# Decay attention followed by a hard-swish MLP on one core: when v is split and loaded, where its maximum stands, and how the MLP's work is shared out over the heads

## The chip, the core and the metric

The kernel runs on one core of one Trainium2 chip. The metric is the device time of one execution in microseconds, the median over runs. The engines are TensorE (PE, with its weight loads as PEld), VectorE (DVE), ScalarE (ACT), GpSimd (POOL) and SyncE (SP), whose queue issues all of this kernel's DMAs. Each engine works through its own instruction stream in order and waits there for what other engines or DMAs owe it.

## What is computed

The reference, cut to what matters (batch 8, 8 heads, 576 tokens, head size 64; then 4608 tokens of width 512 through an MLP of width 2048):

```python
scores = scale * np.matmul(q, k.transpose(0, 1, 3, 2))
cum = np.cumsum(np.log(np.clip(f, 0.0001, 1.0)), axis=-1)
decay = cum[:, :, :, None] - cum[:, :, None, :]
scores = np.where(causal, -1000000000.0, scores + decay)
attn = softmax(scores)                       # max, exp, sum, divide
attn_out = np.matmul(attn, v)
x = attn_out.transpose(0, 2, 1, 3).reshape(B * S, H * D)
h = x @ w_in
g = h * np.clip(h + 3.0, 0.0, 6.0) / 6.0
out = g @ w_out
```

## The kernel before

One program does both halves at once. The attention goes head by head through a list `VH`: four entries of kind A (two heads of batch 0 each, their first 256 queries), eight of kind B (the rest of batch 0) and 56 of kind F, one head each, for batches 1 to 7. "Head 4 of batch 3" below counts both from 0. The MLP works on tiles of 512 tokens, nine in all; tile t needs x from batch t (576 tokens a batch, so a tile ends inside a batch or with it), and so cannot be finished before that batch's last head.

**A head of kind F.** POOL copies q and k (`parts`, tiles TQ and TK), SP copies parts of them (`rests`, L453 and L454, into T7 and T1), POOL subtracts (L455, L458). PE computes the scores in two halves (`rows`, L608 and L611, tile pn). VectorE adds the mask and takes the row maximum (L619, pp and MF), and forms the bias nb (L625). ScalarE takes exp (L631) and a rounded fp16 copy (L645, tile ring); VectorE and POOL subtract for the rest (L648, L654, L659). SP transposes each half by DMA (L666, tile pT). PE multiplies by v (`av`, L691 to L696, tile pav), VectorE divides (L727 to L729) and after two heads splits x into two fp16 halves (xhl, L735). One head later SP transposes these into `xT` (`x_move`, L755).

**v.** A batch's v is loaded into the one buffer `vst` (`load_v`: L359 twice for the first 64 rows of chunk 0, and L360 for the other four chunks of 128 rows). `v_scale` takes the largest absolute value on VectorE in two reduces (L365: chunks 0 to 2, chunks 3 and 4), squares it, joins the partitions on PE and makes a power of two of it. `v_split` then makes two fp16 halves for a pair of heads (L396 on ScalarE, L397 on VectorE). The next load may only overwrite `vst` when all four pairs of the batch are split.

**The MLP's queue.** `units` holds generators of work. `moe_tile` of a tile yields 16 `h_unit`s (12 matmuls L781 to L783 into ph; Relu on ScalarE L791, product on VectorE L794 into r, fp16 copy L795 on ScalarE, remainder L796 on VectorE, both into gT) and then four `out_unit`s (48 matmuls L803 to L805 into po, L814 on ScalarE, L815 to memory). The main loop calls `fill(1)` eight times per head; each adds `rates[0]` to a credit, and units are taken from the queue while there is credit. A whole tile is 64 credits. The rate is 0.6 during kind B, 0.45 in batch 1 and 1.02 from batch 2 on. `done` puts a tile into the queue, right after `x_move` of the last pair of a batch, which happens in the middle of head 1 of the next batch. What remains in the queue runs after the last head, and then tile 8.

**What sets the order.** The loop gives only the program's order. A scheduler then orders each engine's stream by priority and by a simulated timeline, so that an instruction without unfinished inputs may move ahead of earlier ones. `tc.issue_after(x)` ties instructions behind x on its engine; the load of v is tied so behind an early DMA. `keep_in_program_order(y)`, which the change uses, ties y behind the one instruction of its engine that the program gave just before it.

Of the kernel before, what the change touches and what calls it, by code (L numbers as in the profile page):

```python
# [20 lines left out]
def kernel(  # L21
# [10 lines left out]
    nc = tc.nc  # L32
# [3 lines left out]
    B = vS.shape[0]  # L36
    H = NHEAD // B
    NT, DM = out.shape
    DFF = w_in.shape[1]
    P = 128  # L40
# [5 lines left out]
    NFC = DFF // P  # L46
    TT = 512
# [34 lines left out]
    NQK, NL, NST = 3, 2, 3  # L82
    W_RATE = (8, 5, 4)
    H_COST = 1.05
    F_RATE = (0.6, 0.45, 1.02)
    PIN = 0
    PIN0 = 1
    LOW_W = 0
# [6 lines left out]
    QA = 256  # L95
    CA = QA // P
    VH = [("A", g) for g in range(NPAIR)] + [("B", n) for n in range(H)]
# [46 lines left out]
    def v_parts(b):  # L144
        return v0 if b == 0 else [vst[:, 0:3], vst[:, 3:]]
# [34 lines left out]
    def pow2_scale(pm, s_col, i_col, name):  # L180
        pool, tag = (ps_t, "tr") if SV < s_col < SV + B else (ps_m, "mm")
        pt = pool.tile([P, 512], F32, tag=tag, name=f"pt_{name}")
        nc.tensor.matmul(pt[:, 0:1], ones, pm, start=True, stop=True)
        yield
        e = p2.tile([P, 2], F32, tag="ee", name=f"e_{name}")
        nc.vector.tensor_scalar(e[:, 0:1], pt[:, 0:1], 2.0 ** -100, None, op0=ALU.max)
        ei = e.bitcast(I32)
        nc.vector.tensor_scalar(
            ei[:, 1:2], ei[:, 0:1], 24, 23, op0=ALU.logical_shift_right, op1=ALU.logical_shift_left
        )  # L190
        si = SC.bitcast(I32)
        nc.vector.tensor_scalar(
            si[:, s_col:s_col + 1], ei[:, 1:2], -1.0, float(204 << 23), op0=ALU.mult, op1=ALU.add
        )
        nc.vector.tensor_scalar(
            si[:, i_col:i_col + 1], ei[:, 1:2], 1.0, float(50 << 23), op0=ALU.mult, op1=ALU.add
        )
        yield

    def scol(c):  # L200
        return SC[:, c:c + 1]
# [160 lines left out]
    def v_scale(b):  # L362
        pm = p2.tile([P, 2], F32, tag="pm", name=f"vm{b}")
        for i, t in enumerate(v_parts(b)):
            nc.vector.tensor_reduce(  # L365
                pm[:, i:i + 1], t.rearrange("p c (h e) -> p (c h) e", e=D + 1)[:, :, 0:D],
                axis=AX.XY, op=ALU.max, apply_absolute_value=True,
            )
            yield
        nc.vector.tensor_tensor(pm, pm, pm, op=ALU.mult)  # L370
        nc.vector.tensor_tensor(pm[:, 0:1], pm[:, 0:1], pm[:, 1:2], op=ALU.max)
        yield from pow2_scale(pm[:, 0:1], SV + b, IV + b, f"v{b}")
# [15 lines left out]
    def v_split(g):  # L388
        b, hp = divmod(g, NPAIR)
        t = v16[:, g % NV16]  # L390
        if g < NPAIR + NV16:
            nc.vector.memset(t[:, :, :, D:D + 1], 1.0)
        for j in range(2):
            o = (2 * hp + j) * (D + 1)
            src = vst[:, :, o:o + D]
            nc.scalar.activation(t[:, :, j, 0:D], src, AF.Copy, scale=scol(SV + b))  # L396
            nc.vector.scalar_tensor_tensor(  # L397
                t[:, :, j, D + 1:VW], src, scol(SV + b), t[:, :, j, 0:D],
                op0=ALU.mult, op1=ALU.subtract,
            )  # L400

    def load_x(v):
        kind, n = VH[v]
        t = ST[v % NST]
        if kind == "A":
            nc.sync.dma_start(
                t[:, 0:2 * QA].rearrange("p (h s) -> p h s", h=2),
                qk[2 * n:2 * n + 2, :, 0:QA].rearrange("h p s -> p h s"),
            )
        else:  # L410
            nc.sync.dma_start(t, qk[n])

    def load_c(v):
        kind, n = VH[v]
        t = TK[v % NQK].bitcast(F32)[D:D + 2]
        if kind != "A":
            nc.sync.dma_start(t[:, 0:S], scr[n])
            if kind == "F":
                nc.sync.dma_start(TQ[v % NQK].bitcast(F32)[D + 2:D + 4, 0:S], scr[n])
        elif n >= 2:  # L420
            nc.sync.dma_start(
                t[:, 0:2 * QA].rearrange("r (h s) -> r h s", h=2),
                scr[2 * n:2 * n + 2, :, 0:QA].rearrange("h r s -> r h s"),
            )
        else:
            for h in range(2):
                d = nc.sync.dma_start(
                    t[:, h * QA:(h + 1) * QA], cs.bitcast(F32)[2 * n + h:2 * n + h + 1, :, 0:QA]
                )
            if PIN0:  # L430
                small.append(d.ins)
# [9 lines left out]
    def parts(v):  # L441
        i = v % NQK
        s = ST[v % NST]
        nq, nk, q0 = spans(v)
        one = dict(scalar1=1.0, scalar2=0.0, op0=ALU.mult, op1=ALU.add)
        nc.gpsimd.tensor_scalar(TK[i][0:D, 0:nk], s[D:, 0:nk], **one)
        nc.gpsimd.tensor_scalar(TQ[i][0:D, 0:nq], s[0:D, q0:q0 + nq], **one)
# [370 lines left out]
    def moe_tile(t, c0=0, c1=TT):  # L818
        for fc in range(NFC):
            j, new = divmod(fc, NFC // NG)  # L820
            if new == 0 and t < B and c0 == 0:
                while j not in w_in_done:
                    next(w_in_q, None)
                moe_scale_in(t, j)
            yield from h_unit(t, fc, c0, c1)
        if t == 0:
            for _ in wq:
                pass
        if t < B and c0 == 0:
            moe_scale_out(t)  # L830
        for s in range(c0 // P, c1 // P):
            yield from out_unit(t, s)
# [43 lines left out]

    units = []

    credit, rates = [0.0], [1.0]

    def w_step():
        with tc.high_priority(offset=-LOW_W):
            next(wq, None)

    def fill(k):
        credit[0] += k * rates[0]
        while credit[0] >= 1 and units:
            with tc.high_priority(offset=-LOW_M):
                r = next(units[0], 0)
            if r == 0:  # L890
                units.pop(0)
            else:
                credit[0] -= r
        credit[0] = min(credit[0], 1.0)

    def one(*a):
        yield from moe_tile(*a)

    def done(v):
        kind, n = VH[v]  # L900
        if kind == "A":
            if n == NPAIR - 1:
                units.append(one(0, 0, QA))
            return
        b, h = divmod(n, H)
        if h == H - 1:
            units.append(one(b, QA if b == 0 else 0, TT))
            if b == B - 1:
                units.append(one(B))

    prev = None
    pend_x = None
    vq = v_scale(0)
    for i, (kind, n) in enumerate(VH):
        b, h = divmod(n, H)
        if kind == "A":
            b = h = 0
        wn = W_RATE["ABF".index(kind)]
        rates[0] = F_RATE[0] if kind == "B" else F_RATE[min(b, 2)]
        ahead = i + 2 < NV  # L920
        if i + 3 < NV:
            load_x(i + 3)
        if ahead:
            load_c(i + 2)
        if b + 1 < B and h == 6:
            load_v(b + 1)
        if b and h % 2 == 1 and h < H - 1:
            v_split((n + 1) // 2)
        sg = rows(i) if kind == "F" else scores(i)
        front = ahead and VH[i + 2][0] != "F"  # L930
        next(sg)
        if i + 1 < NV:
            rests(i + 1)
        if ahead:
            parts(i + 2)
        fill(1)
        if b + 1 < B and h == 7:
            vq = v_scale(b + 1)
        next(vq, None)
        fill(1)  # L940
        ph = next(sg)
        if i + 1 < NV and VH[i + 1][0] != "F":
            max_rows(i + 1)
        for _ in range(wn // 2):
            w_step()
        fill(1)
        next(vq, None)
        next(sg, None)
        fill(1)
        if pend_x is not None:  # L950
            x_move(pend_x)
            done(pend_x)
            pend_x = None
        if front:
            natural(i + 2, 0)
        fill(1)
        if b + 1 < B and h == 7:
            for _ in vq:
                pass
            if b:  # L960
                v_split((n + 1) // 2)
        for _ in range(wn - wn // 2):
            w_step()
        next(sg, None)
        fill(1)
        if front:
            natural(i + 2, 1)
        fill(1)
        if prev is not None:
            av(*prev)  # L970
            if VH[prev[0]][0] == "A" or VH[prev[0]][1] % 2 == 1:
                pend_x = prev[0]
        if n == H:
            v_split(n // 2)
        fill(1)
        prev = (i, ph)
    rates[0] = 1.0
    av(*prev)
    fill(4)
# [40 lines left out]
```

## Time and profile before

| | |
|---|---|
| median of 3 runs | 1084.57 us (1083.75 to 1087.27) |
| profiled execution | 1083.28 us, span from first to last instruction 1081.5 us |
| mean granted TensorE clock | 0.982 of full |
| busy: PE, DVE, ACT, POOL | 1010.1, 719.7, 610.1, 413.1 us |
| DMA | 133.74 MB, 124 GB/s on average |

How to read it: busy time is time in which an instruction of the engine was under way. Matmuls are pipelined and their ends are modelled, so a PE that is busy all of a stretch may still have been a little slower than it could be; the granted clock, which a throttle sets, is given beside it as a share of full speed. In rows by time windows each engine's busy time stands with the number of its instructions in that window. "A <- B" in rows of waits says that A's engine stood still until B was finished; "issue" means that the profile shows nothing that it waited for.

### The profile page before, as it was taken

Reading aid. Unit: us, or ns where it says so; the run is one execution under the profiler, and the core shown is the slowest. Engines: PE = TensorE matmul, PEld = TensorE weight load, DVE = VectorE, ACT = ScalarE, POOL = GpSimd, SP = SyncE. Lnnn points to the kernel's source line nnn. Section 1 sums busy time; section 2 is a strip of 40 time slices with the busy share of each in tenths; the row PEclk is TensorE's granted clock in tenths of the full one; section 3 lists DMA queues with packets and bytes.
Section 4 is the critical chain, followed back from the end, with each engine's and each line's share of the span. In section 5 each row is a group of like instructions: output and inputs, shape, how many; then the busy total and the mean of one; then the engine's idle time right before and its main releaser. Section 6 shows DMA issues by size and latency. Waiting matters only on the chain.

```text
span 1081.5 us, 20281 instructions
## 1 busy us (share of the span) xinstructions
PE 1010.1 (93%) x7074; PEld 577.4 (53%) x7074; DVE 719.7 (67%) x1887; ACT 610.1 (56%) x1285; POOL 413.1 (38%) x505
## 2 busy tenths in 40 slices
PE   2799977988999999999999989999999999999998
PEld 2567854755555555555555545555555555444443
DVE  7869899876885688468865795689668841510520
ACT  4778656845764577356754674477447841621520
POOL 7344455335434445444544444454445420000000
PEclk9989989999999999999999999999999999999999
DMA  8866547767756666667576856675666651000001
GB/s 258 277 172 194 150 105 134 179 127 150 156 114 141 140 146 118 137 129 164 108 139 138 164 113 130 146 166 114 128 140 128 106 112 46 1 10 30 1 1 39
DMA packets 261650, 133.74 MB, mean 124 GB/s; under 512 B 229444, under 2 KB 231036, under 8 KB 261548
## 3 DMA queue, kind: packets, MB, share of 16 engines
q1 hardware_dynamic: 261548, 132.45, 54.7%
q8 instruction: 56, 0.92, 0.3%
q14 instruction: 46, 0.38, 0.1%
HBM read 47.93 MB, written 9.73 MB: 53 GB/s over the span
## 4 chain that ended last, share of the span: by engine, by line
PE 64%; DVE 12%; DMA 9%; issue 5%; ACT 5%; SPq 2%; POOL 2%; DVEq 0%; POOLq 0%; ACTq 0%
PE po L803 10%; PE po L804 10%; PE po L805 10%; PE ph L781 7%; PE ph L782 7%; PE ph L783 7%; DMA vst<-in_vS_dram 3%; PE pn L611 3%; PE pn L608 2%; DVE pp L619 2%; DVE ring L648 2%; DMA T<-TK 1%; DVE gT L796 1%; DMA w<-in_w_in_dram 1%; DVE r L794 1%
## 5 line engine op out<-in xcount | busy, mean ns | idle before, releaser
L781 PE MATMUL ph<-xT,w 128*128 128x512 f16 (+1 forms) x640 | 231.2, 363 | 14.5 <-DVE r L794 9.1
L782 PE MATMUL ph<-xT,w 128*128 128x512 f16 (+1 forms) x640 | 230.2, 363 | 0.0
L783 PE MATMUL ph<-xT,w 128*128 128x512 f16 (+1 forms) x640 | 230.0, 363 | 0.0
L631 ACT ACTIVATE pp<-pp,nb 128x192 f32<-128x192 f32 x280 | 138.5, 552 | 148.8 <-DVE nb L625 145.8
L804 PE MATMUL po<-w,gT 128*128 128x512 f16 x576 | 216.3, 381 | 6.1 <-DVE w L294 6.1
L805 PE MATMUL po<-w,gT 128*128 128x512 f16 x576 | 215.9, 381 | 0.0
L803 PE MATMUL po<-w,gT 128*128 128x512 f16 x576 | 213.6, 381 | 1.1 <-ACT o L814 0.8
L648 DVE TENSOR_TENSOR ring<-pp,ring 128x128 f16<-128x128 f32 (+2 forms) x216 | 131.5, 622 | 84.1 <-ACT ring L645 83.2
L791 ACT ACTIVATE r<-ph,bias_r,SC 128x256 f32<-128x256 f32 (+7 forms) x272 | 144.4, 570 | 28.6 <-PE ph L783 27.9
L794 DVE SCALAR_TENSOR_TENSOR r<-r,ph 128x512 f32<-128x512 f32 (+1 forms) x160 | 100.1, 627 | 88.9 <-ACT r L791 88.6
L458 POOL TENSOR_TENSOR T<-ST,T 64x576 fp32r<-64x576 f32 (+1 forms) x68 | 101.2, 1488 | 143.2 <-DMA T<-TK 133.4
L619 DVE CUSTOM_DVE_ANT_0 pp<-pn,W 128x192 f32<-128x192 f32 x280 | 122.9, 482 | 20.6 <-PE pn L611 16.6
L796 DVE TENSOR_TENSOR gT<-r,gT 128x512 f16<-128x512 f32 (+1 forms) x160 | 118.3, 743 | 27.4 <-ACT gT L795 26.6
L795 ACT CAST gT<-r 128x512 f16<-128x512 f32 (+1 forms) x160 | 91.8, 575 | 75.9 <-DVE r L794 75.8
L608 PE MATMUL pn<-TK,TQ 68*128 68x192 f32 x336 | 124.1, 383 | 5.8 <-issue 5.0
L611 PE MATMUL pn<-T,T 128*128 128x192 f32 x336 | 113.5, 368 | 4.3 <-POOL T L458 4.3
L645 ACT CAST ring<-pp 128x192 f16<-128x192 f32 x280 | 112.9, 452 | 0.0
L455 POOL TENSOR_TENSOR T<-ST,TQ 64x576 fp32r<-64x576 f32 (+2 forms) x68 | 97.6, 1435 | 24.8 <-PE pn L611 18.2
L654 POOL TENSOR_TENSOR ring<-pp,ring 128x128 f16<-128x128 f32 x96 | 61.5, 641 | 105.5 <-ACT ring L645 83.7
L782 PEld LDWEIGHTS <-w 128*128 128x128 f16 x640 | 62.7, 99 | 65.8 <-issue 20.9
L805 PEld LDWEIGHTS <-gT 128*128 128x128 f16 x576 | 56.8, 99 | 74.9 <-issue 13.7
L781 PEld LDWEIGHTS <-w 128*128 128x128 f16 x640 | 63.1, 99 | 62.2 <-issue 14.3
(136 smaller groups left out, 1703.4 us busy)
## 6 DMA issues: line engine op xcount, KB each, us to landing
ST<-in_qk_dram SPq DMA_DIRECT2D x64, 288.0 KB
T<-TK SPq DMA_DIRECT2D x64, 144.0 KB
out_dram<-o SPq DMA_DIRECT2D x36, 256.0 KB
ring<-in_w_out_dram SPq DMA_DIRECT2D x16, 512.0 KB
T<-TQ SPq DMA_DIRECT2D x56, 144.0 KB
vst<-in_vS_dram SPq DMA_DIRECT2D x7, 1040.0 KB
ring<-in_w_in_dram SPq DMA_DIRECT2D x9, 512.0 KB
w<-in_w_in_dram SPq DMA_DIRECT2D x7, 512.0 KB
```

The costliest lines, as they stand in the source:

```text
L608: nc.tensor.matmul(dst, TQ[i][0:D + 4, qs], TK[i][0:D + 4, a:e], start=True, stop=False)
L611: nc.tensor.matmul(dst, T7[j][:, qs], T1[j][:, a:e], start=False, stop=True)
L619: nc.vector.tensor_tensor_reduce(pp[:r, w:w + kw], pn[:r, o:o + kw], W[:r, 4 * P + r - kw:4 * P + r], 1.0, -3.0e38, ALU.add, ALU.max, accu ...
L631: nc.scalar.activation(x_, x_, AF.Exp, bias=nb[:r, e0 + x:e0 + x + 1], scale=0.125)
L648: eng.tensor_tensor(hl[:r, a:a + c * P], pp[:r, at[c] + 64:at[c] + kw], hl[:r, h0[c] + 64:h0[c] + kw], op=ALU.subtract,)
L781: nc.tensor.matmul(ph, w1[0][:, cc, fs_], xh, start=(cc == 0), stop=False)
L782: nc.tensor.matmul(ph, w1[0][:, cc, fs_], xl, start=False, stop=False)
L783: nc.tensor.matmul(ph, w1[1][:, cc, fs_], xh, start=False, stop=(cc == NCC - 1))
L791: nc.scalar.activation(r[:, a:e], ph[:, a:e], AF.Relu, bias=bias_r, scale=scol(A1 + NG * b + fc * NG // NFC))
L803: nc.tensor.matmul(po, gT[:, 0, fc, ts_], w2[:, fc, 0, :], start=(fc == 0), stop=False)
L804: nc.tensor.matmul(po, gT[:, 0, fc, ts_], w2[:, fc, 1, :], start=False, stop=False)
L805: nc.tensor.matmul(po, gT[:, 1, fc, ts_], w2[:, fc, 0, :], start=False, stop=(fc == NFC - 1))
```

## The change

Three things change in the order in which the program gives its work, and one in how much of the queue a head takes.

- v is split for pairs 1, 2 and 3 of a batch in heads 1, 2 and 4 (before: 1, 3 and 5), and the next batch's v is loaded in head 5 (before: 6).
- The two reduces of `v_scale` are each tied behind the VectorE instruction that the program gave just before.
- A tile of batches 1 to 7 joins the queue at the start of the next head, no longer in the head in which its last x is moved.
- From batch 2 on the rate is no longer 1.02, but what is left in the queue less 8 credits, shared evenly over the fills up to the next tile, held between 0.5 and 1.25.

```diff
-    F_RATE = (0.6, 0.45, 1.02)
+    F_RATE = (0.6, 0.45)
...
-            nc.vector.tensor_reduce(
+            most = nc.vector.tensor_reduce(
                 pm[:, i:i + 1], t.rearrange("p c (h e) -> p (c h) e", e=D + 1)[:, :, 0:D],
                 axis=AX.XY, op=ALU.max, apply_absolute_value=True,
             )
+            if b:
+                tc.keep_in_program_order(most)
...
+    credit, rates, left = [0.0], [1.0], [0.0]
+    TILE = NFC * 2 * H_COST + TT // P * NFC // 2 * (2.0 - H_COST)
+    RESERVE = 8.0
+    def queue(unit, columns):
+        units.append(unit)
+        left[0] += TILE * columns / TT
+    def even(h):
+        heads = (1 - h) % H + 1
+        return min(max((left[0] - RESERVE) / (8 * heads), 0.5), 1.25)
...
                 credit[0] -= r
+                left[0] -= r
...
-        if b + 1 < B and h == 6:
+        if b and h in (1, 2, 4):
+            v_split(n // 2 + 1 if h > 1 else (n + 1) // 2)
+        if b + 1 < B and h == 5:
             load_v(b + 1)
-        if b and h % 2 == 1 and h < H - 1:
-            v_split((n + 1) // 2)
+        if moved is not None:
+            done(moved)
+            moved = None
+        rates[0] = F_RATE[0] if kind == "B" else F_RATE[b] if b < 2 else even(h)
...
             x_move(pend_x)
-            done(pend_x)
+            if VH[pend_x][0] == "F":
+                moved = pend_x
+            else:
+                done(pend_x)
```

What this makes of the streams is shown at three places of batch 4; batches 3, 5 and 6 look alike. Lines of the changed kernel are two higher there (L619 becomes L621, L781 becomes L783, and so on). In the names, pp_39 and pT_39 belong to head 3 of batch 4, pp_40 to head 4, r_3_6 to tile 3, vm5 to the maximum of batch 5's v.

VectorE at the maximum over the next batch's v, before:

```order
L619 ISA pp_39_1_6104,MF1_109<-pn_39_1_6099,W_88 128x320
L619 ISA MF1_109 128x1
L619 ISA pp_39_1_6104,MF1_109<-pn_39_1_6099,W_88 128x448
L619 ISA MF1_109 128x1
L365 TENSOR_REDUCE vm5_6760<-vst_112 128x1 x2
L648 TENSOR_TENSOR ring0_123<-pp_39_0_6050,ring0_123 128x128
```

and now:

```order
L621 ISA pp_40_0_6120,MF0_108<-pn_40_0_6111,W_88 64x64
L621 ISA MF0_108 64x1
L796 SCALAR_TENSOR_TENSOR r_3_3_0_6096<-r_3_3_0_6096,ph_3_3_0_6037 128x512
L627 TENSOR_SCALAR nb_40_6110<-MF0_108 128x3
L798 TENSOR_TENSOR gT_116<-r_3_3_0_6096,gT_116 128x512
L365 TENSOR_REDUCE vm5_6673<-vst_112 128x1
L621 ISA pp_40_1_6175,MF0_108<-pn_40_1_6170,W_88 128x320
```

Both reduces stood together behind head 3's maxima; now the first stands between the two halves of head 4's (in batches 3 and 5 behind the second half), and the second, not shown, among head 7's rows.

SP at the load of that v, before:

```order
L666 DMA_TRANSPOSE pT_38_5858<-ring1_124 128x13x128
L411 DMA ST1_104<-in_qk_dram 128x576
L666 DMA_TRANSPOSE pT_38_5858<-ring2_125 128x12x128
L359 DMA vst_112<-in_vS_dram 64x520 x2
L360 DMA vst_112<-in_vS_dram 128x4x520
L755 DMA_TRANSPOSE xT1_118<-xhl_36_5838 128x2x64
```

and now:

```order
L668 DMA_TRANSPOSE pT_39_5923<-ring0_123 128x13x128
L419 DMA TK0_96<-decay_dram 2x576
L421 DMA TQ0_93<-decay_dram 2x576
L668 DMA_TRANSPOSE pT_39_5923<-ring1_124 128x12x128
L455 DMA T71_102<-TQ2_95 64x576
L456 DMA T11_100<-TK2_98 64x576
L360 DMA vst_112<-in_vS_dram 128x4x520
```

The small part of the load (L359, not in the second piece) stays behind head 2's transposes; the large part moved behind those of head 3 and two copies for a later head.

PE at the first matmuls of tile 3, before, in head 1 of batch 4 (v = 37):

```order
L608 MATMUL pn_37_1_5748<-TK1_97,TQ1_94 128x320
L611 MATMUL pn_37_1_5748<-T11_100,T71_102 128x320
L608 MATMUL pn_37_1_5748<-TK1_97,TQ1_94 128x448
L611 MATMUL pn_37_1_5748<-T11_100,T71_102 128x448
L781 MATMUL ph_3_0_0_5765<-xT0_117,w10_113 128x512
```

and now, in head 3 (v = 39):

```order
L610 MATMUL pn_39_0_5925<-TK0_96,TQ0_93 128x256
L613 MATMUL pn_39_0_5925<-T11_100,T71_102 128x256
L610 MATMUL pn_39_0_5925<-TK0_96,TQ0_93 64x64
L613 MATMUL pn_39_0_5925<-T11_100,T71_102 64x64
L783 MATMUL ph_3_0_0_5949<-xT0_117,w10_113 128x512
```

The tile starts nearly two heads later; the transposes of its last x stay where they were on SP, around head 1.

More of the change, by code (lines that the diff above doesn't have):

```diff
@@ L877 @@
     units = []
-    credit, rates = [0.0], [1.0]
+    credit, rates, left = [0.0], [1.0], [0.0]
[7 more added lines that the diff above has]
+        return min(max((left[0] - RESERVE) / (8 * heads), 0.5), 1.25)
     def w_step():
@@ L902, in done @@
             if n == NPAIR - 1:
-                units.append(one(0, 0, QA))
+                queue(one(0, 0, QA), QA)
             return
@@ L906, in done @@
         if h == H - 1:
-            units.append(one(b, QA if b == 0 else 0, TT))
+            queue(one(b, QA if b == 0 else 0, TT), TT - QA if b == 0 else TT)
             if b == B - 1:
-                units.append(one(B))
+                queue(one(B), TT)
     prev = None
-    pend_x = None
+    pend_x = moved = None
     vq = v_scale(0)
@@ L918 @@
         wn = W_RATE["ABF".index(kind)]
-        rates[0] = F_RATE[0] if kind == "B" else F_RATE[min(b, 2)]
         ahead = i + 2 < NV
@@ L976 @@
         prev = (i, ph)
+    if moved is not None:
+        done(moved)
     rates[0] = 1.0
```

## Prediction

> **What bounds the kernel now.** I read the page first, then the chain, then the heads by time windows, then waits, then single rows.
>
> ```profile
> span 1081.5 us, 20281 instructions
> PE 1010.1 (93%) x7074; PEld 577.4 (53%) x7074; DVE 719.7 (67%) x1887; ACT 610.1 (56%) x1285; POOL 413.1 (38%) x505
> PE po L803 10%; PE po L804 10%; PE po L805 10%; PE ph L781 7%; PE ph L782 7%; PE ph L783 7%; DMA vst<-in_vS_dram 3%; PE pn L611 3%; PE pn L608 2%; DVE pp L619 2%; DVE ring L648 2%; DMA T<-TK 1%; DVE gT L796 1%; DMA w<-in_w_in_dram 1%; DVE r L794 1%
> ```
>
> TensorE is busy 93% of the span and carries the chain; the one transfer with a share worth naming is the load of v, 3%. So moving matmuls about gains nothing: only time in which PE stands still, or runs at a lower clock, can be had back. I cut the trace at the first score matmul (L608) of heads, so that one row is one batch (1 to 6), then heads 0 to 6 of batch 7, then the rest. Columns: length, then busy us (instructions) of PE, PEld, DVE, ACT, POOL, granted clock, DMA share, GB/s.
>
> ```profile
> 135.80:236.90 101.10, 82.70 (x733) 57.67 (x732) 92.08 (x255) 65.34 (x144) 48.63 (x49) 0.95 0.67 139
> 236.90:347.50 110.60, 106.15 (x794) 59.30 (x791) 80.40 (x217) 68.07 (x148) 48.76 (x64) 0.97 0.66 139
> 347.50:457.90 110.40, 107.73 (x802) 59.15 (x801) 77.15 (x200) 64.44 (x140) 50.59 (x63) 0.98 0.65 133
> 457.90:567.20 109.30, 106.42 (x807) 59.09 (x805) 82.47 (x227) 68.72 (x149) 51.61 (x64) 1.00 0.65 136
> 567.20:680.60 113.40, 107.95 (x804) 59.21 (x803) 79.05 (x211) 66.83 (x145) 52.86 (x66) 0.98 0.66 138
> 680.60:788.40 107.80, 106.08 (x803) 58.65 (x801) 79.32 (x198) 64.51 (x140) 50.27 (x63) 1.00 0.66 137
> 788.40:879.50 91.10, 91.10 (x695) 50.53 (x694) 68.92 (x186) 60.62 (x132) 41.71 (x51) 1.00 0.62 124
> 879.50:1081.50 202.00, 197.52 (x992) 91.13 (x988) 52.51 (x91) 61.13 (x103) 2.00 (x3) 1.00 0.09 23
> ```
>
> Batches 3 to 6 hold the same work and differ by up to 5.6 us; batch 7, which loads no v, has no PE idle at all. Head by head only two differ: head 1 (first five rows, batches 3 to 7) and head 4 (next five).
>
> ```profile
> 362.70:373.30 10.60, 10.10 (x88) 6.07 (x86) 6.42 (x17) 5.27 (x13) 4.23 (x7) 1.00 0.54 121
> 473.30:485.30 12.00, 10.06 (x86) 6.05 (x85) 7.84 (x24) 6.35 (x14) 5.93 (x9) 1.00 0.55 129
> 582.40:594.70 12.30, 10.08 (x87) 6.03 (x86) 6.59 (x19) 6.01 (x14) 6.73 (x9) 1.00 0.60 145
> 695.80:705.70 9.90, 9.90 (x86) 5.97 (x85) 5.52 (x16) 4.56 (x11) 3.75 (x5) 1.00 0.55 107
> 803.80:813.70 9.90, 9.90 (x86) 5.97 (x85) 6.21 (x19) 5.29 (x12) 3.75 (x5) 1.00 0.35 79
> 399.70:417.60 17.90, 15.73 (x106) 8.20 (x104) 15.86 (x40) 13.33 (x29) 8.01 (x9) 0.90 0.55 101
> 511.80:526.70 14.90, 13.96 (x104) 7.60 (x103) 13.11 (x35) 11.87 (x27) 6.87 (x8) 1.00 0.55 117
> 621.10:640.10 19.00, 15.77 (x106) 8.12 (x104) 17.10 (x41) 13.38 (x30) 8.21 (x9) 0.91 0.48 100
> 732.20:748.10 15.90, 14.18 (x106) 7.70 (x104) 15.04 (x37) 12.53 (x28) 8.19 (x10) 1.00 0.67 125
> 840.20:854.00 13.80, 13.80 (x104) 7.51 (x103) 12.22 (x30) 11.12 (x26) 8.51 (x10) 1.00 0.73 126
> ```
>
> Against the undisturbed 9.9 us, head 1 loses 0.7 + 2.1 + 2.4 + 0 = 5.2 us; against 13.8 us, head 4 loses 4.1 + 1.1 + 5.2 + 2.1 = 12.5 us. What PE waited for from 270 to 880 us (first two rows), and DVE from 240 to 880 us (total, times, longest):
>
> ```profile
> PE ph L781 <- DVE r L794: 8.1, 5, 3.2
> PE ph L781 <- DMA xT<-xhl: 4.7, 3, 2.2
> DVE vm L365 <- DMA vst<-in_vS_dram: 11.2, 4, 4.2
> DVE vm L365 <- issue: 3.1, 1, 3.1
> ```
>
> Head 1 loses to the transposes of x, which the first matmuls of a new tile need; head 4 to VectorE, which holds r and gT back while its maximum over v waits for the load.
>
> In head 4 of batches 3 and 5 PE idles 17.90 - 15.73 = 2.2 and 3.2 us, and the granted clock of the whole head is 0.90 and 0.91: 17.9 x 0.10 = 1.8 and 19.0 x 0.09 = 1.7 us more. Idle plus clock is the loss. Idle of 0.9 to 1.9 us in one head left the clock at 1.00. [...]
>
> **The change, part by part.** Every engine executes the same set of instructions before and after, so it adds and removes no work; it moves it.
>
> *A tile joins the queue at the next head's start.* The first ph matmul of a tile moves from behind head 1's scores to behind those of head 3, while the transposes stay at head 1 on SP. Two heads of 12 us stand against waits of at most 2.2 us. The cover is the rest of the tile before, which the even share stretches over these heads; were it gone, the waits would return at 5.2 us. I take all 5.2. Bounds 0 and 5.2.
>
> *Load of v and its maximum.* This is not what the words of the change suggest. SP issues L359 where it did, behind head 2's pT, but L360, four fifths of the load, now stands a head later, behind both pT transposes of head 3 and two copies (L455, L456). The first of the two reduces moves from head 3's to head 4's L619 rows in batches 3 to 6; it is tied to one VectorE instruction, which itself stands in head 4. Only the second goes to head 7. So the race with the load stays; when does each arrive?
>
> ```profile
> L365 DVE TENSOR_REDUCE vm<-vst x14: 1208/1480/1753, 124.1 to 731.6; 128x1 f32<-128x1536 f32 x7, 128x1 f32<-128x1024 f32 x7
> ```
> ```profile
> 503.88 0.58 SPq L360 DMA_DIRECT2D vst<-in_vS_dram  x1
> 509.58 2.88 DVE L365 TENSOR_REDUCE vm<-vst 128x1 f32<-128x1536 f32 x2 [3.13 <-issue]
> ...
> 840.34 1.16 SPq L453 DMA_DIRECT2D T<-TQ  x1
> 841.54 0.59 SPq L454 DMA_DIRECT2D T<-TK  x1
> 842.23 1.83 SPq L666 DMA_TRANSPOSE pT<-ring  x1
> ...
> 840.07 1.12 DVE L648 TENSOR_TENSOR ring<-pp,ring 128x256 f16<-128x256 f32 x2
> 846.38 0.68 DVE L796 TENSOR_TENSOR gT<-r,gT 128x512 f16<-128x512 f32 x1
> 847.39 0.61 DVE L619 CUSTOM_DVE_ANT_0 pp<-pn,W 128x448 f32<-128x448 f32 x1
> ```
>
> Batch 4 gives the load's time: from L360's issue at 503.88 to the reduce at 509.58, 5.7 us. Batch 7 gives a clean head 3 to 4. L648 ends at 841.2; the transpose (1.83), the copies (1.16 and 0.59, less if the first finds its data) and gaps bring L360 to 844.2 to 844.9, its data to 849.9 to 850.6. VectorE reaches the reduce's new place at 847.1 (behind gT, batches 4 and 6) or 848.0 (behind L619, batches 3 and 5). It waits 1.9 to 3.5 us, middle 2.7, and then reduces 1.75 us: 4.45 us. Now it is (11.2 - 1.2 of batch 2 + 3.1) / 4 = 3.3 us of waiting and 2.9 of reducing: 6.2 us. That is 1.75 us shorter per batch, so PE's idle of 2.2, 0.9, 3.2 and 1.7 us shrinks to about 0.4, 0, 1.5 and 0, below the gaps that cost clock. Since in two batches the reduce now also stands ahead of head 4's own L619 pair, I put the remaining loss at 5 us rather than 2. Gain 7.5; bounds 0 (waits as now) and 12.5 (load in time). The second reduce, 1.2 us in head 7, meets landed data; VectorE was busy 12.2 of 13.8 us in batch 7's head 4, without a loss on PE, so a head has room for it and it costs nothing. If that slack were gone it is 4 x 1.2 = 5 us.
>
> *Splits of v at heads 1, 2 and 4.* On VectorE they stand within some rows of where they did, the last in head 2 as before: 0.
>
> *Even shares from batch 2 on.* Batch 2's eight heads take 294 of the queue's matmuls where they took 369; 84 more run behind the last head's first score, 978 for 894. The last row of the batches' table holds those 894 in 202 us, so 84 are at most 19 us there, at clock 1.00 as in full heads; moving them costs nothing by itself. But batch 2 is where heads run thin:
>
> ```profile
> 251.30:258.10 6.80, 6.80 (x71) 4.51 (x70) 4.80 (x17) 3.19 (x7) 3.69 (x6) 1.00 0.68 157
> 258.10:264.40 6.30, 5.68 (x33) 3.44 (x31) 5.49 (x14) 2.74 (x7) 4.08 (x6) 1.00 0.23 43
> 264.40:282.20 17.80, 14.10 (x96) 7.77 (x95) 12.48 (x30) 12.35 (x27) 7.26 (x10) 0.81 0.88 178
> ```
>
> Heads 1 and 2 with 18 queue matmuls each run full; then head 3 idles 3.7 us and runs at 0.81, 17.8 x 0.19 = 3.4: with head 2's 0.6, 7.7 us lost. Between the scores of heads 0 to 4 stood 54, 18, 18, 36 and 60 queue matmuls; now 15, 57, 18, 24 and 36. Thin heads remain, but in two places. I take 2 us as gained, near the existing loss; bounds +7.7 and -5.
>
> *Batches 0 and 1.* Rows shuffle by a few places and v is asked for some rows earlier; batch 1 is tied to VectorE, 92.1 of 101.1 us. I take 0, bounds 3 either way.
>
> Sum: the profiled execution took 1083.28 us, 1.3 below the median of 1084.57. 1083.3 - 5.2 - 7.5 - 2 = 1068.6; on the median's footing 1070.
>
> **Rivals.** *All stalls go* (load in time, batch 2 smooth): 1083.3 - 5.2 - 12.5 - 7.7 + 1.3 = 1059. For it: batch 7's clean heads. Against: the race worked out above.
>
> *The maximum waits as before*: L360 a head later, the reduce a head later, nothing won: 1083.3 - 5.2 - 2 + 1.3 = 1077, 1079 without batch 2's part. For it: the rows of the new order. Against: 1.2 us of reducing does leave head 4.
>
> *Batch 2 starves, and it is slower*: heads 0, 2, 3 and 4 each lose what head 3 loses now, 7.1 us, 28.4 in place of 7.7: 1083.3 + 20.7 - 5.2 - 7.5 + 1.3 = 1093. It decides once batch 2 loses over 7.7 + 12.7 = 20.4 us. For it: less filler, and idle of 3.7 us was followed by 0.81. Against: 6.8 and 6.3 us heads above. [...]
>
> A later load is part of none: L360 now passes copies that read what POOL writes.
>
> ```profile
> SPq L411 <- POOL T L458: 89.3, 37, 6.3
> SPq L454 <- POOL TK L446: 0.6, 1, 0.6
> ```
>
> The copies hardly ever waited for POOL (0.6 us); the load of q and k (L411), which did, stands behind L360.
>
> **How the numbers follow.** Forecast 0.50, own range 1064 to 1075; all stalls go 0.17; maximum waits as before 0.21; starving 0.07; some other wait that eats the gain 0.05, about no change. A measurement here tells 0.3%, 3.3 us, from no change: under 1081.3 is faster. Faster: 0.50 + 0.17 + 0.15 of the third = 0.82; same 0.06 + 0.05 = 0.11; slower 0.07. The range 1058 to 1081 leaves out starving, the last case and a few hundredths at each end.
>
> **What would show it.** Head 1 of batches 3 to 5 near PE's busy time, with no wait for xT; VectorE still waiting 2 to 3.5 us for vst in head 4 of batches 3 to 6, with PE idle under 1.5 us and clock 1.00 there; no such wait in batch 2; the stretch from the last head's first score longer by up to 19 us. It is wrong if those waits on vst are gone (then lower), if head 4 keeps clocks near 0.9, or if batch 2 loses over 10 us.

## The result, and the profile after

The change made the kernel slower: 1099.88 us median of 4 runs (1096.02 to 1102.07) against 1084.16 us (1082.56 to 1087.27) on the same chip, a ratio of 1.0141 with a 95% interval of 1.0115 to 1.0167. The prediction said 1070 us and faster. The profiled execution took 1102.07 us, 18.8 us more than that of before, and its span grew by as much. From its page, the span and the engines' busy time:

```profile
span 1100.3 us, 20286 instructions
...
PE 1018.9 (93%) x7074; PEld 582.7 (53%) x7074; DVE 729.8 (66%) x1887; ACT 611.4 (56%) x1285; POOL 411.1 (37%) x505
```

The shares of busy time hardly moved; they cannot show where 18.8 us went. The table by stages can: batches 1 to 6, heads 0 to 6 of batch 7, the rest, cut at first score matmuls (now L610) as in the prediction, with the same columns.

```profile
142.90:242.80 99.90, 82.37 (x732) 57.58 (x732) 91.20 (x246) 63.32 (x139) 49.57 (x49) 0.93 0.65 138
242.80:343.60 100.80, 92.47 (x718) 52.77 (x715) 79.50 (x219) 66.83 (x147) 51.88 (x65) 0.95 0.74 145
343.60:455.90 112.30, 106.20 (x801) 58.52 (x797) 82.17 (x212) 66.64 (x144) 50.29 (x65) 0.98 0.65 135
455.90:564.40 108.50, 107.77 (x803) 59.53 (x801) 79.38 (x208) 67.00 (x144) 51.71 (x65) 0.99 0.61 135
564.40:680.30 115.90, 109.50 (x807) 60.26 (x805) 82.47 (x215) 66.96 (x144) 49.92 (x63) 0.97 0.61 132
680.30:789.30 109.00, 106.81 (x805) 58.98 (x803) 81.11 (x211) 67.07 (x144) 49.37 (x64) 1.00 0.65 138
789.30:880.20 90.90, 90.90 (x693) 50.14 (x692) 66.00 (x181) 56.90 (x125) 39.74 (x50) 1.00 0.64 124
880.20:1100.30 220.10, 215.63 (x1076) 99.45 (x1072) 57.45 (x100) 66.92 (x115) 2.40 (x4) 1.00 0.09 24
```

Against before, row by row: the stretch ahead of batch 1 is 7.1 us longer, batch 1 1.2 shorter, batch 2 9.8 shorter, batches 3 to 6 differ by +1.9, -0.8, +2.5 and +1.2, batch 7 0.2 shorter, the end 18.1 longer. Together 18.8. The number behind PE's busy time is its instructions: batch 2 does 76 fewer, the end 84 more. To see what a head loses whatever its share, I use a line that heads without PE idle lie on (in batch 7 before, 9.9 us with 33 queue matmuls and 13.8 us with 51): length = 2.85 us + 0.2156 us x queue matmuls. What a head takes beyond it I call its loss; single thin heads, with 18 to 30 queue matmuls, come out up to 1.3 us below the line. By it batch 2, with 75 queue matmuls fewer, should have become 16.2 us shorter and lost 6.5 of that: its loss went from 8.2 to 14.7. Batches 3 to 6 lost 18.5 before and lose 25.2 now.

Head 1 of batches 3 and 5 (first two rows), then head 4 of batches 3 to 7:

```profile
356.80:370.00 13.20, 13.20 (x103) 7.29 (x101) 9.04 (x26) 6.13 (x13) 8.12 (x11) 1.00 0.63 126
578.50:592.90 14.40, 13.38 (x102) 7.29 (x101) 10.95 (x26) 6.12 (x13) 10.35 (x13) 1.00 0.71 167
396.40:413.50 17.10, 13.21 (x97) 7.09 (x95) 8.68 (x23) 7.98 (x18) 6.41 (x8) 0.93 0.71 172
512.10:524.00 11.90, 11.90 (x96) 6.72 (x95) 7.55 (x20) 6.40 (x14) 6.26 (x8) 1.00 0.76 199
620.70:639.30 18.60, 13.22 (x97) 7.09 (x95) 7.64 (x22) 7.49 (x17) 6.40 (x8) 0.92 0.70 165
735.10:748.60 13.50, 12.14 (x97) 6.83 (x95) 8.63 (x21) 6.40 (x14) 6.76 (x8) 1.00 0.81 199
844.10:855.20 11.10, 11.10 (x93) 6.38 (x91) 9.78 (x25) 8.70 (x20) 6.22 (x8) 1.00 0.32 65
```

Head 1 is full, or nearly (5.1 us of loss before, 1.2 now). Head 4 still stands still for 3.9 and 5.4 us in batches 3 and 5 and for 1.4 in batch 6, and its clock falls to 0.93 and 0.92. The waits of PE from 270 to 880 us, then VectorE's for v from 240 to 885 us:

```profile
PE ph L783 <- DVE r L796: 11.6, 5, 5.4
PE pav L693 <- DMA pT<-ring: 4.7, 4, 1.9
PE pn L613 <- POOL T L460: 2.8, 2, 2.2
PE pt_v L183 <- DVE vm L373: 2.4, 2, 2.2
```
```profile
DVE vm L365 <- DMA vst<-in_vS_dram: 22.7, 4, 8.8
```

The wait for xT is gone, that for r has grown from 8.1 to 11.6 us, and VectorE waits 22.7 us for v. Why, shows SP's queue in batch 3 and VectorE beside it (first column the start, second the duration, in brackets the idle time before):

```profile
388.98 1.54 SPq L359 DMA_DIRECT2D vst<-in_vS_dram  x2
390.60 0.54 SPq L817 DMA_DIRECT2D out_dram<-o  x1
391.24 6.83 SPq L757 DMA_TRANSPOSE xT<-xhl  x5
398.23 1.31 SPq L668 DMA_TRANSPOSE pT<-ring  x1
...
400.95 1.44 SPq L668 DMA_TRANSPOSE pT<-ring  x1
...
404.00 0.59 SPq L360 DMA_DIRECT2D vst<-in_vS_dram  x1
```
```profile
393.77 1.12 DVE L650 TENSOR_TENSOR ring<-pp,ring 128x256 f16<-128x256 f32 x2
...
402.76 0.08 DVE L621 DVE_READ_ACCUMULATOR2_ANT MF<- 128x1 f32 x1
409.46 1.22 DVE L365 TENSOR_REDUCE vm<-vst 128x1 f32<-128x1024 f32 x1 [6.61 <-DMA vst<-in_vS_dram]
410.59 0.68 DVE L796 SCALAR_TENSOR_TENSOR r<-r,ph 128x512 f32<-128x512 f32 x1
```

Five transposes of x hold SP for 6.8 us ahead of head 3's pT, and L360 stands behind that. VectorE is at the maximum at 402.8; L360 goes out only at 404.0, and its data are there 5.5 us later; r (L796) and with it PE stand behind the maximum. In batches 4 to 6 VectorE waits 3.4, 8.8 and 3.9 us in the same place.

The batches are not alike in this. From the end of head 3's last L650 to L360 it is 404.00 - 394.89 = 9.1 us in batch 3 and 10.9 us in batch 5, but 4.0 and 4.6 us in batches 4 and 6; head 4 loses 5.1, 6.7, 0 and 1.5 us. Batch 4 has the same five transposes, but SP is through with them 2.0 us before that L650 ends, and not 3.2 us behind it:

```profile
502.20 6.35 SPq L757 DMA_TRANSPOSE xT<-xhl  x5
...
514.48 0.59 SPq L360 DMA_DIRECT2D vst<-in_vS_dram  x1
```
```profile
509.41 1.12 DVE L650 TENSOR_TENSOR ring<-pp,ring 128x256 f16<-128x256 f32 x2
...
519.99 1.22 DVE L365 TENSOR_REDUCE vm<-vst 128x1 f32<-128x1024 f32 x1 [3.38 <-DMA vst<-in_vS_dram]
```

Why SP reaches them later in batches 3 and 5 was not settled. One more reading: the reduce in head 4 is the second (128x1024). The tie holds it behind one instruction of the MLP's queue, which itself runs heads early.

### The profile page after: what moved, and what is told of

The parts are those of the page before. It is cut to its first block, busy times and chain, and to the rows that moved or that the text cites. A ratio compares the mean times of both kernels' runs of the same rounds, so it can differ in the third digit from the quotient of the medians.

```text
span 1100.3 us, 20286 instructions
## 1 busy us (share of the span) xinstructions
PE 1018.9 (93%) x7074; PEld 582.7 (53%) x7074; DVE 729.8 (66%) x1887; ACT 611.4 (56%) x1285; POOL 411.1 (37%) x505
## 4 chain that ended last, share of the span: by engine, by line
PE 61%; DVE 11%; DMA 10%; ACT 6%; issue 6%; POOL 3%; SPq 2%; DVEq 0%; ACTq 0%; POOLq 0%
PE po L805 10%; PE po L806 10%; PE po L807 10%; PE ph L783 7%; PE ph L784 7%; PE ph L785 7%; PE pn L613 3%; PE pn L610 3%; DVE pp L621 2%; ACT pp L633 2%; DMA pT<-ring 2%; DVE ring L650 2%; DMA T<-TK 1%; DMA ring<-in_w_out_dram 1%; SPq L757 1%
## 5 line engine op out<-in xcount | busy, mean ns | idle before, releaser
L783 PE MATMUL ph<-xT,w 128*128 128x512 f16 (+1 forms) x640 | 228.8, 365 | 14.6 <-DVE r L796 14.0
L784 PE MATMUL ph<-xT,w 128*128 128x512 f16 (+1 forms) x640 | 227.9, 363 | 0.0
L785 PE MATMUL ph<-xT,w 128*128 128x512 f16 (+1 forms) x640 | 227.1, 363 | 0.0
L650 DVE TENSOR_TENSOR ring<-pp,ring 128x128 f16<-128x128 f32 (+2 forms) x216 | 136.4, 642 | 67.9 <-ACT ring L647 67.2
L796 DVE SCALAR_TENSOR_TENSOR r<-r,ph 128x512 f32<-128x512 f32 (+1 forms) x160 | 100.1, 626 | 109.0 <-ACT r L793 108.6
L621 DVE CUSTOM_DVE_ANT_0 pp<-pn,W 128x192 f32<-128x192 f32 x280 | 123.1, 482 | 28.0 <-PE pn L613 23.6
L610 PE MATMUL pn<-TK,TQ 68*128 68x192 f32 x336 | 128.7, 396 | 0.6 <-DVE MF L621 0.5
L613 PE MATMUL pn<-T,T 128*128 128x192 f32 x336 | 116.8, 374 | 6.3 <-POOL T L460 6.3
L784 PEld LDWEIGHTS <-w 128*128 128x128 f16 x640 | 63.2, 99 | 71.3 <-issue 22.3
L785 PEld LDWEIGHTS <-w 128*128 128x128 f16 x640 | 63.3, 99 | 66.6 <-issue 9.7
L783 PEld LDWEIGHTS <-w 128*128 128x128 f16 x640 | 62.3, 99 | 58.6 <-issue 11.6
```

The costliest lines, as they stand in the source:

```text
L610: nc.tensor.matmul(dst, TQ[i][0:D + 4, qs], TK[i][0:D + 4, a:e], start=True, stop=False)
L613: nc.tensor.matmul(dst, T7[j][:, qs], T1[j][:, a:e], start=False, stop=True)
L621: nc.vector.tensor_tensor_reduce(pp[:r, w:w + kw], pn[:r, o:o + kw], W[:r, 4 * P + r - kw:4 * P + r], 1.0, -3.0e38, ALU.add, ALU.max, accu ...
L650: eng.tensor_tensor(hl[:r, a:a + c * P], pp[:r, at[c] + 64:at[c] + kw], hl[:r, h0[c] + 64:h0[c] + kw], op=ALU.subtract,)
L783: nc.tensor.matmul(ph, w1[0][:, cc, fs_], xh, start=(cc == 0), stop=False)
L784: nc.tensor.matmul(ph, w1[0][:, cc, fs_], xl, start=False, stop=False)
```

## The experiments

Theory 1: the maximum, put into head 4 without a firm place, races the load there, and that costs. Rival 2: the even shares cost by themselves, by thin heads in batch 2 and by moved waits. Rival 3: the earlier splits hold ScalarE, and PE waits for that. The first four runs, the next four and the last three stood beside the kernel before on one chip each (1084.4, 1082.2 and 1082.8 us there); "loss" is the sum over batches 2 to 6 in the profiled execution, before 26.7 us, after 39.9.

**pin_only**: the kernel before, with the ties alone.

```diff
+            if b:
+                tc.keep_in_program_order(most)
```

> The kernel before with the two reduces of the maximum tied as in the change, nothing else. In its order both reduces of batches 3 to 6 stand at head 7 and the load stays behind head 2's transposes. Theory 1 (the race of the maximum with the load in head 4 is what costs): head 4 of batches 3 to 6 loses nothing, 12.5 us of the kernel before come back, about 1072 us. Rival 2 (thin filler is what costs): the queue's shares are as before, so about 1084 us less the idle of PE behind VectorE alone, 1076 us. Rival 3 (earlier splits hold ScalarE): nothing of it is here, no statement beyond 1084 us.

Measured 1070.68 us (1067.62 to 1072.07), ratio 0.9879 (0.9839 to 0.9919). Without the shares the ties do hold both reduces at head 7, the load stays behind head 2, VectorE never waits for v from 240 us on, and head 4 loses nothing in any batch. All that PE waits for from 230 to 870 us:

```profile
PE ph L783 <- DMA xT<-xhl: 4.7, 2, 2.6
PE pav L693 <- DMA pT<-ring: 1.9, 2, 1.2
PE pn L610 <- DVE MF L621: 1.0, 1, 1.0
```

So one part of the change is worth 13 us, and another spoils it.

**shares_only**: the kernel before, with the rates of `even(h)`. (`moved` is left out: beside the shares it changes no place in the program's order, since the queue then never runs dry from batch 2 on and `done` only adds to its end.)

```diff
-        rates[0] = F_RATE[0] if kind == "B" else F_RATE[min(b, 2)]
+        rates[0] = F_RATE[0] if kind == "B" else F_RATE[b] if b < 2 else even(h)
```

> The kernel before with the even shares alone. In its order L360 moves behind head 3's transposes and both reduces stand in head 4, as in the change. Theory 1: the waits on vst in head 4 grow to 3 to 9 us as in the change and cost 13 to 16 us in batches 3 to 6, the transposes of x cost nothing (5 us back): 1082 to 1086 us, and with 6 us lost in batch 2 up to 1092. Rival 2: batches 2 to 7 lose through thin heads wherever the maximum stands: 1095 us or more. Rival 3: no splits are moved, 1080 us.

Measured 1099.13 us, ratio 1.0149 (1.0115 to 1.0183): all of the change's cost. In the order L360 stands behind head 3's pT, both reduces in head 4. Theory 1 had set 1082 to 1086 us, at most 1092, and rival 2 1095 or more, so by the time rival 2 fits; but 25.1 of the 29.3 us lost in batches 3 to 6 are lost in their heads 4, where the maximum waits, and not in thin heads. VectorE's wait for v from 240 to 885 us and PE's largest from 230 to 870 us:

```profile
DVE vm L365 <- DMA vst<-in_vS_dram: 30.4, 5, 9.2
```
```profile
PE ph L781 <- DVE r L794: 22.5, 6, 8.1
```

**splits_only**: the kernel before, with the splits in heads 1, 2 and 4 and the load in head 5.

```diff
-        if b + 1 < B and h == 6:
+        if b and h in (1, 2, 4):
+            v_split(n // 2 + 1 if h > 1 else (n + 1) // 2)
+        if b + 1 < B and h == 5:
```

> The kernel before with the splits of v in heads 1, 2 and 4 and the load in head 5, nothing else. Load and maximum stand in batches 3 to 6 where they stood. Theory 1: 1084 us, 3 us either way for batch 1 and 2. Rival 2: 1084 us. Rival 3: waits of ScalarE's splits for pav grow from 12 to some 30 us and cost 5 to 10 us: 1090 us.

Measured 1083.29 us, ratio 0.9999 (0.9975 to 1.0022). Rival 3 is out for the splits by themselves.

**max_at_7**: the changed kernel, the second reduce tied behind the first and not behind a queue instruction. Both then stand at head 7.

```diff
+            if b and i == 0:
+                tc.keep_in_program_order(most)
+                first = most
+            if b and i == 1:
+                tc.add_manual_dep(most.ins, first.ins.name, ..., reason="behind_first")
```

> The changed kernel with one edit: the second reduce is tied behind the first, so that both stand at head 7. Theory 1: the waits on vst (22.7 us of VectorE in batches 3 to 6) vanish and 13 of the 15.7 us come back: 1087 us. Rival 2: only PE's idle behind VectorE (11 us in the heads 4) matters if filler was lacking anyway, so less than half comes back: 1094 us or more. Rival 3: no difference, 1100 us.

Measured 1085.02 us, ratio 1.0016 (0.9993 to 1.0038): 14.9 us below the changed kernel. No wait for v is left and head 4 loses at most 1 us in batches 3 to 6. But it is still 14 us above pin_only: batch 2 loses 15.9 us, and from 230 to 870 us PE now waits mostly for something else:

```profile
PE pav L700 <- DMA pT<-ring: 13.1, 11, 3.3
```

**shares_max_at_7** (the kernel before, the shares, both reduces at head 7) and **splits_max_at_7** (the kernel before, the splits, both at head 7), the tie as in max_at_7. The first, and the last two runs below, keep `moved`, which is without effect there.

> The kernel before with the even shares and with both reduces at head 7 (the second tied behind the first); splits and load are given as before. Theory 1 (what is left of the loss beside the race is thin heads at the start of batch 2, and these come from the splits' new places, which leave 15 queue matmuls in head 0): heads 0 to 4 of batch 2 hold 30, 21, 45, 33, 45, so batch 2 loses 3 to 6 us and the waits for xT are gone: 1068 to 1072 us. Rival 2 (the shares themselves cost, since 84 matmuls run behind the last head): 1080 to 1085 us, as with all parts.

> The kernel before with the new places of splits and load and with both reduces at head 7; the rate stays 1.02. Heads 0 to 4 of batch 2 hold 15, 57, 9, 93, 48 queue matmuls. Theory 1: batch 2 loses 12 to 16 us as in the change, batches 3 to 6 lose only what the waits for xT take (5 to 9 us): 1079 to 1084 us. Rival 2: no shares, so as with the ties alone, 1071 us.

Measured 1079.8 us (ratio 0.9986, 0.9956 to 1.0015) and 1070.58 us (0.9896, 0.9864 to 0.9928). The second is the changed kernel without its shares and `moved`, and as fast as pin_only; batch 2 loses 5.9 us, so by themselves the splits do not thin it, as theory 1 had it. The first is 9 us above pin_only: rival 2 holds for that much. Theory 1 missed both (1068 to 1072 and 1079 to 1084 us). Head 1 has no waits for xT any more, but head 4 of batches 4 and 6 has waits of 2.4 and 3.0 us for pT. SP's queue ahead of the first (the pT is head 3's, which PE multiplies by in head 4), and PE:

```profile
488.14 6.35 SPq L764 DMA_TRANSPOSE xT<-xhl  x5
...
495.09 1.47 SPq L675 DMA_TRANSPOSE pT<-ring  x1
...
498.73 1.51 SPq L675 DMA_TRANSPOSE pT<-ring  x1
```
```profile
504.19 0.20 PE L700 MATMUL pav<-v,pT 128*128 128x65 f16 x1 [2.43 <-DMA pT<-ring]
```

The wait for the transposes of x was not won but passed on: pT stands behind all five.

**ties_rate_040**: pin_only with 0.40 in place of 0.45 for batch 1, so that more of tile 0 is left to batch 2.

```diff
-    F_RATE = (0.6, 0.45, 1.02)
+    F_RATE = (0.6, 0.40, 1.02)
```

> The kernel before with the two ties of the change and a rate of 0.40 in place of 0.45 in batch 1. Batch 1 takes 15 queue matmuls fewer, which leaves heads 0 to 4 of batch 2 with 51, 39, 51, 45, 51 in place of 54, 18, 18, 36, 60. Theory 1: batch 2 loses 0 to 1 us where the ties alone lose 6.4, all else as there: 1064 to 1066 us. Rival 2: fewer queue matmuls inside the first batches mean more behind them, 1074 us.

Measured 1065.72 us (1060.96 to 1072.01), ratio 0.9852 (0.9802 to 0.9902): faster than both kernels and the lowest median here, though its interval overlaps that of pin_only. Batch 2 takes 51, 39, 51, 45, 51, 48, 45 and 54 queue matmuls per head and loses 0.3 us. One wait of PE is left from 230 to 870 us:

```profile
PE ph L783 <- DMA xT<-xhl: 4.1, 2, 2.7
```

**load_together**: the changed kernel with `load_v` at a high priority, which brings L360 right behind L359.

```diff
-            load_v(b + 1)
+            with tc.high_priority(offset=2000):
+                load_v(b + 1)
```

> The changed kernel with a higher priority for the load of v alone. In its order L360 stands right behind L359, behind head 2's transposes, and the loose reduce moves with it to head 3's rows; heads 0 to 4 of batch 2 hold 60, 57, 30, 39, 30. Theory 1: VectorE waits for vst in batches 3 to 6 by 3 us as in the kernel before, with 1.2 us of reducing: heads 3 and 4 lose 4 to 8 us over the four batches in place of 13; batch 2 loses under 6 us: 1080 to 1085 us. Rival 2: 1095 us or more.

Measured 1094.64 us, ratio 1.0133 (1.0085 to 1.018). Theory 1 missed (1080 to 1085 us); rival 2's 1095 or more is nearer. The loose reduce moved ahead with the load, to head 3 (in batch 5 just into head 4), and still waits for it:

```profile
DVE vm L365 <- DMA vst<-in_vS_dram: 15.9, 4, 6.5
```

An earlier load helps little, 5 us, while the maximum has no place of its own. Batch 1 takes 66 queue matmuls less here than in the changed kernel and batch 2 as many more, so this run differs from it in the filler too.

**reserve_2**: the changed kernel with one number changed. It shifts where in a batch a tile ends; nothing ahead of batch 2 depends on it.

```diff
-    RESERVE = 8.0
+    RESERVE = 2.0
```

> The changed kernel with one number changed: RESERVE 2 in place of 8, so that the queue in its steady state stands some 6 columns' worth further on. In the order L360 then stands right behind L359 at head 2, ahead of the five (now four) xT transposes, both reduces stand at head 7, and the last xT transpose stands behind the first half of head 3's pT; the last head keeps 936 matmuls instead of 978. Theory 1 (what costs is where the tile's end falls against the load and the transposes on SP: the race in head 4, and pT behind five xT): both go, no vst wait over 2 us, head 4's losses in batches 3 to 6 under 1 us each: 1068 to 1077 us. Rival 2 (the even shares cost by themselves, 9 to 15 us over the ties alone, whatever the phase): 1079 to 1086 us.

Measured 1080.26 us (1075.26 to 1084.16), ratio 0.9974 (0.9948 to 1.0001), 20 us below the changed kernel; above theory 1's 1068 to 1077, inside rival 2's 1079 to 1086. The tile now begins in head 2, L360 goes out 1.2 us after L359 and ahead of the transposes (batch 4), and both reduces stand at head 7 by the same ties:

```profile
491.13 1.14 SPq L359 DMA_DIRECT2D vst<-in_vS_dram  x2
492.32 0.58 SPq L360 DMA_DIRECT2D vst<-in_vS_dram  x1
494.83 5.02 SPq L757 DMA_TRANSPOSE xT<-xhl  x4
500.01 1.47 SPq L668 DMA_TRANSPOSE pT<-ring  x1
```

No wait for v is left; batches 3 to 6 lose 8.1 us in place of 25.2, 6.3 of them in heads 5. Batch 2 loses 11.1. Theory 1 has the mechanism right in batches 3 to 6, rival 2 has the remainder, which is batch 2.

**shares_max_7_reserve_2** (shares_max_at_7 with RESERVE 2) and **shares_040_reserve_2** (that with 0.40 for batch 1).

> shares_max_at_7 (shares, both reduces at head 7, the splits as before) with RESERVE 2 in place of 8, which puts the xT transposes of the tile's end ahead of head 3's pT partly and the load back ahead of both. Theory 1: the waits of PE for pT from the ring (9.6 us in 8 waits, 2.4 to 3.0 us in head 4 of batches 4 and 6) go under 3 us in all and no wait for xT comes back: 1066 to 1073 us. Rival 2 (shares cost by themselves): 1077 to 1082 us as before.

> The run before with 0.40 in place of 0.45 for batch 1, which leaves batch 2 more of the queue (27, 27, 51, 42, 48, 48, 45, 48 matmuls a head). Theory 1: as ties_rate_040 (1065.7 us), without its 4 us of waits for xT in head 1 and with up to 3 us in batch 2: 1060 to 1068 us. Rival 2: 1070 to 1078 us.

Measured 1074.34 us (ratio 0.9913, 0.9885 to 0.9941) and 1082.19 us (0.9985, 0.9956 to 1.0013). The first lies between the two ranges: the waits of head 4 are gone, but 1.6 to 2.0 us of loss, waits for pT, stand in head 5 of each batch from 3 to 6. From 230 to 870 us PE waits 5.6 us for pT, not under 3 as theory 1 asked, and one wait of 1.3 us for xT is back. The second missed both ranges. Its batch 2 loses 6.8 us in head 2 and 4.0 in head 5, and head 5 of batch 4 loses 7.9, with a wait of 3.95 us for pT; there VectorE stood 2.8 us for POOL's part of the ring, which POOL reached behind two copies (L455, L456 there) and two subtractions (L464, L467). Whether these come back in each execution was not tried.

By kernel, with the loss of batches 2 to 6 beside the time:

```
                          us       loss b2   loss b3..b6   VectorE waits for v (240 to 885 us)
before                   1084.2      8.2        18.5          11.2
changed                  1099.9     14.7        25.2          22.7
shares_only              1099.1      9.6        29.3          30.4
load_together            1094.6     12.7        18.9          15.9
max_at_7                 1085.0     15.9        10.9           0
splits_only              1083.3      8.8        20.3          13.6
shares_040_reserve_2     1082.2     10.5        14.3          0
reserve_2                1080.3     11.1         8.1           0
shares_max_at_7          1079.8      7.3        15.1           0
shares_max_7_reserve_2   1074.3      4.0         9.0          0
pin_only                 1070.7      6.4         9.4           0
splits_max_at_7          1070.6      5.9         6.4          0
ties_rate_040            1065.7      0.3         5.6           0
```

The losses are of one execution each, the times medians, and the start differs by some us (below), so the two do not add up exactly.

## Why the prediction was wrong

*The step that failed: when L360 goes out.* The prediction took batch 7 as "a clean head 3 to 4" and put L360 3.0 to 3.7 us behind the end of L648 (841.2 to 844.2 or 844.9). Measured it is 9.1 and 10.9 us in batches 3 and 5, and 4.0 and 4.6 in batches 4 and 6. The row that it did not look for is the transposes of x: ahead of head 3's pT five of them stand on SP in batches 3 to 5 and four in batch 6, three in the reference; batches 3 to 5 of the kernel before have five there too. In batches 3 and 5 SP is through with them 3.2 and 5.0 us behind VectorE's last part of the ring, in the other two ahead of it. In the table of engines SP has no column, so the reference looked clean. The load's own time held (5.7 us taken, 5.4 to 6.5 measured). By that step VectorE would wait 1.9 to 3.5 us, measured 6.6, 3.4, 8.8 and 3.9; head 4's loss should have gone from 12.5 to 5 and is 13.3 (5.1, 0, 6.7, 1.5), with 1.9 more in head 5 of batch 5. The term of -7.5 us is about +1, and +3 with head 5. max_at_7 (-14.9 us) shows what that place of the maximum costs, shares_only that the shares put it and the load there.

*How much of the miss that is.* The profile stands 33.5 us above the sum's 1068.6. About 8 us of it is this term, 8.5 batch 2, 6 batches 0 and 1, 1 head 1. About 9 us had no term: heads 0, 2, 3, 5, 6 and 7 of batches 3 to 6 lose 10.5 us together, 1.2 before, and still 9.0 in max_at_7, where the maximum is out of the way.

*Which reduce is loose.* The prediction had the first (1.75 us) in head 4, as had the reading of the order ahead of it; it is the second, 1.22 us. That the first at head 7 costs nothing was nearly right: PE waited 2.2 us for the joined maximum (pt_v, L183) in head 7 of batch 3, which lost 2.8.

*Batch 2.* Taken as 2 us gained, with bounds of 7.7 gained and 5 lost; measured 6.5 us lost (8.2 to 14.7), outside them. The rival that it starves is the right side but not the case: it needed 20.4 us. shares_only has 9.6 there and splits_only 8.8; with both, in the changed kernel, max_at_7 and load_together, it is 12.7 to 15.9. So beside the shares the splits do cost: reserve_2 took 5.9 us more than shares_max_7_reserve_2, which has the splits as before and both reduces at head 7 too, on the same chip, with 7.1 us more lost in batch 2. Why the two together thin it more was not settled.

*Even shares cost nothing by themselves.* Their 84 moved matmuls cost 18.1 us at the end against "at most 19", and batch 2 gave back 9.8 for 75 fewer. The other cost of the shares was not in the working: with both reduces at head 7 they are 9 us slower than the ties alone (1079.8 against 1070.7), for the most part through pT behind the transposes of x: heads 4 lose 8.5 us there and 0.1 in pin_only.

*Right.* The waits for xT in head 1 went, as said; of the 5.2 us 3.9 came in, the rest is a wait of 1.0 us for pT in batch 5. The splits alone are worth nothing. The ties were seen not to hold the maximum, and the race to stay.

*Batches 0 and 1.* Taken as 0, bounds 3; measured 7.1 ahead of batch 1 and -1.2 in it. Of the 7.1, 3.9 stand in the first 480 matmuls, which run in the same order in both kernels. These belong to this execution. The other 3.2 us may not: from the 480th matmul to batch 1 it is 27.2 us in the changed kernel, 27.0 to 27.8 in four of the five other profiles with the splits' new places, 24.7 in the fifth (reserve_2, whose order is the same up to the middle of batch 2), and 23.1 to 24.6 in the seven without them. Up to batch 2 no difference is left to tell: 127.1 us against 125.2 before and up to 128.6 in pin_only.

## What to carry to other kernels

Before a step is timed from a "clean" repetition, compare the queue's rows of both: here the DMA queue had five transposes where the reference had three, what counted was whether it was through with them before VectorE (2.0 us before in batch 4, 3.2 and 5.0 us behind in batches 3 and 5), and a queue has no column in a table of busy time. A tie to "the instruction before" is worth what that instruction's place is worth; tie to the work that must come first, and look where the tied one lands. And when a schedule's rates change, ask which transfers change places: the 84 moved matmuls took 18.1 us at the end, 0.22 us each as in full heads, but the rates put the load behind five transposes and the maximum ahead of the load, and one number (8 to 2) took both back.

## What the runs showed of the hardware

Behind some stops of TensorE the granted clock was half of full for 3.41 us or a multiple of it: in the profile of before from 404.57 to 407.98 us (3.41) and from 268.04 to 274.86 (6.83), in that of the changed kernel from 636.30 to 643.13 (6.83). Windows behind gaps of 5.38 us in the changed kernel (first row), of 3.95 us in shares_040_reserve_2 (second, 0.67 over the window), of 2.43 us in shares_max_at_7 (the next two) and of 2.7 us in ties_rate_040 (the last); the clock is the third value from the end.

```profile
637.08:641.40 4.32, 4.28 (x15) 2.74 (x15) 3.56 (x7) 4.29 (x10) 1.88 (x2) 0.50 0.62 111
```
```profile
529.20:536.20 7.00, 7.00 (x52) 3.36 (x52) 3.68 (x10) 3.70 (x8) 0.20 (x1) 0.67 0.52 98
```
```profile
504.20:505.10 0.90, 0.90 (x30) 0.90 (x31) 0.00 (x0) 0.00 (x0) 0.90 (x1) 1.00 1.02 384
505.10:508.50 3.40, 3.40 (x18) 1.94 (x15) 2.52 (x6) 1.25 (x2) 1.06 (x3) 0.50 1.09 330
```
```profile
474.10:480.00 5.90, 5.88 (x51) 3.58 (x52) 4.68 (x15) 3.19 (x7) 0.91 (x2) 1.00 0.89 188
```

In the changed kernel matmuls of 512 columns started 0.43 us apart at half clock (637.50, 637.93, 638.36 us) and 0.22 us apart at full clock (629.64, 629.85, 630.07 us).

The length of the gap alone did not decide it: the one of 2.43 us was followed by half clock, the one of 2.7 us left it at 1.00. In the profiles of before and of the changed kernel all changes of the granted clock lie multiples of 3.41 us apart, so their records can be cut into intervals of that length. Three pairs of neighbours, the first two of before and the third of the changed kernel:

```profile
401.16:404.57 3.41, 1.24 (x9) 0.73 (x8) 3.41 (x11) 2.58 (x6) 0.56 (x1) 1.00 0.26 56
404.57:407.98 3.41, 3.41 (x10) 1.40 (x8) 3.38 (x10) 2.32 (x5) 0.35 (x1) 0.50 1.25 148
```
```profile
588.88:592.30 3.42, 1.57 (x15) 0.79 (x13) 1.82 (x3) 1.67 (x4) 1.81 (x3) 1.00 0.25 48
592.30:595.71 3.41, 3.03 (x42) 2.04 (x42) 2.08 (x7) 2.17 (x5) 0.80 (x1) 1.00 0.49 126
```
```profile
247.18:250.59 3.41, 1.88 (x19) 1.55 (x17) 0.36 (x2) 1.83 (x5) 1.94 (x4) 1.00 0.84 177
250.59:254.00 3.41, 3.41 (x12) 1.39 (x11) 1.88 (x6) 0.00 (x0) 3.25 (x4) 0.50 1.09 204
```

The first gap, 2.17 us, lies whole in one interval, and half clock followed; the second, 2.22 us, lies in two, with 1.84 and 0.38 us, and the clock stayed at 1.00; the third, 1.53 us, lies whole in one, and half clock followed. From 225 to 875 us of these two profiles seven intervals at full clock had 1.95 us or more of PE idle (1.95 to 3.41), and half clock followed each; of two with 1.53 and 1.85 us it followed the first; behind those with 1.45 us or less it did not come. The prediction's "gaps that cost clock", taken to begin above 1.9 us, were no such bound: its own row of head 1 of batch 5 has 2.2 us of idle at 1.00 (the gap of 2.22 us above), and the 3.7 us of head 3 of batch 2 are two gaps of 1.9 and 1.8.

The start varied between executions: the 480th matmul, behind the same matmuls in the same order, began at 108.2 us (pin_only) to 115.7 us (changed kernel) over thirteen profiles, at 111.8 us in that of before. A difference of a few us between two single profiles says nothing until that stretch has been compared.
